# The bias table left raw, loaded first, and six of its rows made on GpSimd

## The chip, the cores and the metric

The kernel runs on one core of one Trainium2 chip. The metric is the device time of one execution in microseconds (us), lower is better. The core has five engines that run on their own and meet at semaphores: TensorE (PE, with its weight loads PEld), VectorE (DVE), ScalarE (ACT), GpSimd (POOL) and SyncE (SP, which here only issues DMAs).

## The reference

Three blocks run one after the other: attention with a learned relative bias, and two mixer blocks. The change is in the bias alone, so only that part of the reference matters:

```python
# q, k, v: [4, 8, 576, 64]; hidden = 32
pos = np.arange(S)
rel = (pos[:, None] - pos[None, :]).astype(np.float32)
psi_rel = np.log1p(np.abs(rel))
psi_i = np.log1p(np.maximum(pos[:, None].astype(np.float32), 1.0))
x = (psi_rel / psi_i)[..., None]
h = np.maximum(x @ w1 + b1, 0.0)        # [576, 576, 32]
bias = h @ w2                           # [576, 576, 8 heads]
scores = scores + bias.transpose(2, 0, 1)[None, :, :, :]
# softmax over the last axis, times v, then the two mixer blocks
```

For one query row the hidden layer is 32 units by 576 keys. Four query rows fill the 128 partitions.

## The kernel before, in words

A row's logarithms log(1+|i-j|) are a slice of one table, `ttab` (128 partitions by 1152), since they depend on i-j alone. Division by psi_i > 0 is taken out of the maximum: the kernel makes max(w1*t + b1*psi_i, 0) and scales it afterwards. `times_w1` (L311) first turns the table into -w1*t in place, once for the first 640 columns and once for the other 512. Then `hidden(gi)` makes a group of 16 query rows as four tiles X of 128x576, four rows each: three on VectorE as min(-w1*t, b1*psi_i) (L347; the sign and the constant are put right afterwards), the fourth on ScalarE as a true Relu (L349). `bias_product` (L366) multiplies them by w2 on TensorE, eight matmuls into one PSUM tile `bps`; `bias_place` (L379) scales the tile by `over_c` and adds `evb` on ScalarE, and a DMA (L385, L389) carries it to `bias_m` or `bias_t`, where the scores read it. X tiles lie in 12 slots that are used in turn, so a tile waits for the matmuls that read its slot three groups before.

There are 36 groups, in the order of `groups` (the four of the last 64 rows first). Six are made ahead of the attention (loop over `GUP`), between the transposes of k (L398 to L403). The other 30 are spread over the loop `single(n)`, two in each step from n = -3 to n = 11. In step n TensorE does: `ss`, the scores of unit n+3 (L470); transposes z, x and y of unit n (L525, L546, L551); a transposition of q into the `bps` buffer (L425); the products of two groups (L366); `values` of unit n-1 (L570 to L577). VectorE does in step n: `pr` (L476: scores plus bias, and the row minimum `mn`), a reciprocal (L496), a second `pr`, the three X tiles of a group, a copy of y (L556), the three X tiles of a second group, and the add of the values (L451). ScalarE does the exponentials (L489), two `bst` (L379), a copy of q (L435), two X tiles (L349) and copies of z and x. GpSimd adds the epsilon to the row sums (L495) and divides by them (L503: `pr` in one instruction of 576 or in three of 576, 64 and 512). In the steps from -3 to 10 the tiles of the groups 2n+14 and 2n+15 are made, one step ahead of their products.

The order of the work on each engine is the order in which the code is written (a manual schedule); SP issues all DMAs in that order too. The score tiles `ss` and the `bps` tiles share two PSUM buffers: the transposition of q (L425) waits until VectorE has read the first `ss` tile of the step, and the second half of `ss` until ScalarE has emptied the last `bps`.

At the start SP loads `wsm` (w1, b1, w2 and psi_i, 77 KB), then `ttab`'s first 640 columns, then the rest. VectorE multiplies psi_i by b1 (L308) and the table by -w1. TensorE meanwhile multiplies zeros (L230). GpSimd builds the w2 operands and `one_row` (L315 to L329), which the products that give `evb` and `over_c` (L594, L598) wait for.

Of the kernel before, what the change touches and what calls it, by code (L numbers as in the profile page):

```python
# [7 lines left out]
F32 = mybir.dt.float32  # L8
F32R = mybir.dt.float32r
I32 = mybir.dt.int32  # L10
AF = mybir.ActivationFunctionType
ALU = mybir.AluOpType
# [7 lines left out]
def kernel(ctx, tc, ins, consts, out, dbg=None, nb=4, stop=None):  # L20
    nc = tc.nc
    V, S, G, T, D = nc.vector, nc.scalar, nc.gpsimd, nc.tensor, nc.sync

    q, k, v = ins["q"], ins["k"], ins["v"]
    B, H, N, HD = q.shape
    P = 128
# [158 lines left out]
    scale = -1.0 / float(HD) ** 0.5  # L185
# [3 lines left out]
    groups = [it * P // 16 + j for it in order0 for j in range((P if it < NM else TL) // 16)]  # L189
# [22 lines left out]
    first = tc.alloc_tile_pool(name="first", bufs=1, side="right")  # L212


    def spare(t):
        blk = t // ND % 3
        return X[:, t % ND, N * (1 + blk):N * (2 + blk)]

    warm = first.tile([P, 1], F32, name="warm")
    V.memset(warm, 0.0)  # L220
    S.activation(out=warm, in_=warm, func=AF.Exp)

    ND0, WN = 2, 512
    NQ = 2
    NV = (-2, -1, 0, 1)
    zero = first.tile([P, N], F32, tag="st", name="zero", bufs=4)[:, 0:WN]
# [6 lines left out]
    wsm = first.tile([P, SMALL], F32, name="wsm")  # L233
    ttab = first.tile([P, 2 * N], F32, name="ttab")
    TC, SM = N + TL, 2 + H + NI
    D.dma_start(out=wsm[:, 0:SM], in_=consts["tab"][:, 0:SM])
    D.dma_start(out=ttab[:, 0:TC], in_=consts["tab"][:, SMALL:SMALL + TC])
    w1c, b1c = wsm[:, 0:1], wsm[:, 1:2]
    pi, rp = wsm[:, 2 + H:2 + H + NI], wsm[:, 2 + H + NI:SMALL]
    D.dma_start(out=ident, in_=consts["ident"])  # L240
# [45 lines left out]
    def load_q0(it):  # L286
        i = order0.index(it)
        if i < NM:
            t = raw_p.tile([P, N], F32, tag=("kr", "qr")[i % 2], name="qm", bufs=1)
        else:  # L290
            t = first.tile([P, DM], F32, name="qm")
        t = t[:, 0:DM].rearrange("p (h d) -> p h d", h=H)
        w = P if it < NM else TL
        D.dma_start(out=t[0:w], in_=q[0, :, it * P:it * P + w, :].rearrange("h p d -> p h d"))
        for p in range(NP):
            qraw[0, p, it] = t[0:w, 2 * p:2 * p + 2].rearrange("p h d -> p (h d)")
# [3 lines left out]
        out=ktail0[0:TL], in_=k[0, :, NM * P:N, :].rearrange("h p d -> p h d")  # L300
# [6 lines left out]

    V.tensor_scalar_mul(out=pi, in0=pi, scalar1=b1c)  # L308

    def times_w1(j):  # L310
        V.tensor_scalar(out=ttab[:, j], in0=ttab[:, j], scalar1=w1c, scalar2=-1.0, op0=ALU.mult, op1=ALU.mult)  # L311

    times_w1(slice(0, TC))
    w2b = first.tile([P, 4, H], F32, name="w2b")
    G.memset(w2b, 0.0)  # L315
    for g in range(4):
# [6 lines left out]
        out=w2r[:, 0:3].rearrange("k c g h -> k (c g) h"),  # L323
        in_=wsm[0:HID, 2:2 + H].rearrange("k (o h) -> k o h", o=1).to_broadcast([HID, 12, H]),
# [5 lines left out]
    rps = ps_t.tile([P, NI // 4], F32, tag="z", name="rps")  # L330
    over_c = first.tile([P, NI // 4], F32, name="over_c")
    evp = ps_t.tile([P, 1], F32, tag="o", name="evp")
    evb = first.tile([P, 1], F32, name="evb")

    nhid = [0]

    def hidden(gi):

        hs = []
        for c in range(4):  # L340
            hd = spare(nhid[0])
            nhid[0] += 1
            base = N - 1 - 16 * gi - 4 * c
            tt = ttab[:, base:base + N]
            b1i = pi[:, 4 * gi + c:4 * gi + c + 1]
            if c < 3:
                V.tensor_scalar(out=hd, in0=tt, scalar1=b1i, scalar2=None, op0=ALU.min)  # L347
            else:
                S.activation(out=hd, in_=tt, func=AF.Relu, scale=-1.0, bias=b1i)  # L349
            hs.append(hd)  # L350
        return hs

# [9 lines left out]
    def bias_product(gi, hs, ps=None):  # L362
        ps = s_tile("bps") if ps is None else ps
        for c in range(4):
            for hf in range(2):
                T.matmul(  # L366
                    ps[32 * c:32 * c + 32, hf, 0:HN],
                    lhsT=w2b.rearrange("p g h -> p (g h)"),
                    rhs=hs[c][:, hf * HN:(hf + 1) * HN],
                    start=True, stop=True, tile_position=(0, 32 * c),  # L370
                )
        return ps

    def bias_place(gi, ps):
        if gi in early:
            st = early.pop(gi)
        else:
            st = first.tile([P, N], F32, tag="st", name="bst", bufs=4)
        S.activation(  # L379
            out=st.rearrange("p (a n) -> p a n", a=2), in_=ps[:, :, 0:HN], func=AF.Identity, scale=over_c[:, gi:gi + 1],  # L380
            bias=evb,
        )
        i0 = 16 * gi
        if i0 < NM * P:
            D.dma_start(out=bias_m[i0 % P // 16:P:GT, i0 // P], in_=st)  # L385
        else:
            r0 = i0 - NM * P
            for a in range(2):
                D.dma_start(out=bias_t[a * TL + r0 // 16:(a + 1) * TL:TL // 16], in_=st[a:P:2])  # L389

    def k_parts0(p, pool, tag):

        m, tl = kraw.pop((0, p))
        tl = tl[0:TL, 2 * p:2 * p + 2]
        yk = ps_t.tile([P, NM, P], F32, tag="xy"[p % 2], name="yk")
        xk = ps_t.tile([P, TL], F32, tag="zo"[p % 2], name="xk")
        for t in range(NM):
            T.transpose(yk[:, t], m[:, t], ident)  # L398
        T.transpose(xk, tl.rearrange("p h d -> p (h d)"), ident[0:TL, 0:TL])
        kt = pool.tile([P, N], F32, tag="kt" + tag, name="kt", bufs=2)  # L400
        M = NM * P
        S.copy(out=kt[:, 0:M].rearrange("d (p t) -> d p t", t=NM), in_=yk.rearrange("d t p -> d p t"))
        V.tensor_copy(out=kt[:, M:N], in_=xk)  # L403
        keys[0, p] = kt
# [15 lines left out]
    def q_turn(n, zq):  # L420

        b, p, it = units[n]
        w = P if it < NM else TL
        if b == 0:
            T.transpose(zq[:, 0:w], qraw.pop((b, p, it)), ident[0:w, 0:w])  # L425
        else:
            queries[n] = turned(b, p)[:, it * P:it * P + w]

    def q_out(n, zq):
        b, p, it = units[n]  # L430
        if b > 0:
            return
        w = P if it < NM else TL
        t = hl_p.tile([P, P], F32, tag="q0", name="q0", bufs=5)[:, 0:w]
        S.copy(out=rows(t, w), in_=dealt(zq[:, 0:w], w))  # L435
        queries[n] = t
# [152 lines left out]
    def hide(gi):  # L589
        if gi < GALL:  # L590
            hs[gi] = hidden(groups[gi])
# [3 lines left out]
        evp, lhsT=w2r.rearrange("k c g h -> k (c g h)"), rhs=b1c[0:HID], start=True, stop=True  # L595
# [4 lines left out]
            tile_position=(0, 32 * c),  # L600
        )
    hide(1)
    V.tensor_scalar_mul(out=evb, in0=evp, scalar1=-1.0 / scale)
    V.tensor_scalar_mul(out=over_c, in0=rps, scalar1=1.0 / scale)
    hide(2)

    for gi in range(GUP):
        if gi == NQ:
            load_q0(order0[1])
        if gi == 2:  # L610
            times_w1(slice(TC, 2 * N))
        if gi > 0:
            bias_place(groups[gi - 1], bps)
            hide(gi + 2)
        bps = bias_product(gi, hs.pop(gi))
        if gi >= GUP - NP:
            p = gi - (GUP - NP)
            k_parts0(p, hl_p if p < 2 else first, "" if p < 2 else "x")
        if gi >= GUP - 2:
            u = gi - (GUP - 2)  # L620
            zq = ps_t.tile([P, P], F32, tag="z", name="zq")
            q_turn(u, zq)
            q_out(u, zq)
    bias_place(groups[GUP - 1], bps)
    gnext = GUP

# [97 lines left out]
    def single(n):  # L724
# [22 lines left out]
        for gi, ps in zip(gs, bp):  # L747
            bias_place(groups[gi], ps)
            if gi == gs[0]:
                q_out(n + 5, zq)  # L750
# [367 lines left out]
    with tc.tile_pool(name="sgw", bufs=1, reuse_waits="tile") as sw, tc.tile_pool(  # L1118
        name="sg", bufs=1, reuse_waits="tile"
# [313 lines left out]
```

## Time and profile before

| | |
|---|---|
| median of 3 runs | 873.35 us (873.16 to 873.83) |
| the profiled execution: its time | 873.12 us |
| its span in the profile | 871.2 us |
| busy PE / PEld / DVE / ACT / POOL | 99% / 88% / 71% / 48% / 26% of the span |
| granted TensorE clock, mean | 1.00 |

1.92 us of the profiled execution lie outside the span. The busy shares are means over unlike stages: the bias groups are made in the first 92 us, where all of VectorE, ScalarE and TensorE are close to full, while the mixers after 300 us are TensorE's alone. The part that the change touches is therefore read in stretches of 5 to 20 us, and by which engine each one waits for.

### The profile page before, as it was taken

To read this page: it belongs to the slowest core of one execution; us is meant where nothing else is said; L and a number is where in the kernel's file an instruction comes from. 1 tells how busy PE (TensorE), PEld (TensorE's weight loads), DVE (VectorE), ACT (ScalarE), POOL (GpSimd) and SP (SyncE) were. 2 spreads that over 40 slices of the span, in tenths; PEclk is the share of its full clock that TensorE was granted. 3 is DMA by queue.
4 is the path that set the end of the run, shared out by engine and by line. 5 is a ranking of instruction groups with operands and counts; after the bars stand their busy time and mean duration, and the time that the engine had idled before them with its cause. 6 is when DMAs were issued, how large, how long until landed. Compare 5 with 4: busy or idle time off the path is not lost.

```text
span 871.2 us, 22145 instructions
## 1 busy us (share of the span) xinstructions
PE 861.0 (99%) x8962; PEld 763.8 (88%) x8962; DVE 622.5 (71%) x1429; ACT 420.5 (48%) x955; POOL 229.5 (26%) x440
## 2 busy tenths in 40 slices
PE   9999999999999999999999999999999999999998
PEld 4466788888888898999999999999998989889996
DVE  7899788888887689899735353422118989887756
ACT  7999888888888634343322121211115522322310
POOL 1345567676767200000000000000002512322230
PEclk9999999999999999999999999999999999999999
DMA  7965554444432222243402001000051001010002
GB/s 191 197 137 130 126 101 78 80 96 90 82 72 59 62 66 82 73 124 118 122 1 73 25 25 44 6 1 0 1 83 49 26 0 50 2 60 2 1 13 96
DMA packets 123990, 57.55 MB, mean 66 GB/s; under 512 B 104177, under 2 KB 112497, under 8 KB 123889
## 3 DMA queue, kind: packets, MB, share of 16 engines
q1 hardware_dynamic: 123728, 56.01, 26.6%
q8 instruction: 70, 1.15, 0.5%
q14 instruction: 32, 0.25, 0.1%
q10 hardware_dynamic: 160, 0.13, 0.1%
HBM read 38.62 MB, written 4.72 MB: 50 GB/s over the span
## 4 chain that ended last, share of the span: by engine, by line
PE 86%; DVE 9%; ACT 2%; issue 1%; DMA 1%; SPq 0%; DVEq 0%; ACTq 0%
PE a L1064 17%; PE pg L900 17%; PE ss L470 9%; PE pu L1231 5%; PE o L570 5%; PE ps L1253 5%; PE po L1284 4%; PE pv L1178 4%; PE x L546 4%; PE y L551 3%; PE bps L366 3%; PE o L571 2%; PE z L525 2%; PE pu L932 1%; PE ph L646 1%
## 5 line engine op out<-in xcount | busy, mean ns | idle before, releaser
L1064 PE MATMUL a<-g,c 128*128 128x384 f32 x864 | 161.5, 334 | 0.0
L1064 PEld LDWEIGHTS a<-g,c 128*128 128x128 f32 x864 | 151.1, 188 | 0.0
L907 DVE SCALAR_TENSOR_TENSOR g<-pg,g 128x384 fp32r<-128x384 f32 x72 | 40.0, 556 | 146.7 <-ACT g L906 146.7
L503 POOL TENSOR_SCALAR pr<-pr,sm 128x576 f32<-128x576 f32 (+2 forms) x208 | 129.8, 640 | 47.0 <-DVE sm L496 38.8
L900 PE MATMUL pg<-u,c 128*128 128x384 f32 x720 | 134.5, 334 | 0.0
L900 PEld LDWEIGHTS pg<-u,c 128*128 128x128 f32 x720 | 125.7, 188 | 0.1
L906 ACT ACTIVATE g<-pg 128x384 fp32r<-128x384 f32 x72 | 35.3, 491 | 182.5 <-PE pg L900 175.0
L489 ACT ACTIVATE pr<-pr,mn 128x576 f32<-128x576 f32 x144 | 112.2, 780 | 6.7 <-DVE mn L476 4.5
L476 DVE CUSTOM_DVE_ANT_0 pr<-ss,bias_m 128x576 f32<-128x576 f32 x128 | 94.5, 749 | 19.4 <-PE ss L470 17.0
L62 POOL TENSOR_TENSOR y<-X,y 128x576 fp32r<-128x576 f32 x4 | 6.1, 1543 | 362.2 <-ACT y L61 362.2
L570 PEld LDWEIGHTS o<-xA,vm 64*64 64x64 f32 x1280 | 69.9, 133 | 11.2 <-issue 5.6
L570 PE MATMUL o<-xA,vm 64*64 64x128 f32 (+1 forms) x1280 | 78.8, 261 | 0.0
L1019 DVE STREAM_TRANSPOSE res<-X 32x256 f32<-32x256 f32 (+1 forms) x176 | 68.2, 387 | 2.9
L571 PE MATMUL o<-yA,vm 64*64 64x128 f32 x1024 | 68.0, 272 | 0.0
L470 PE MATMUL ss<-kt,X 64*64 64x288 f32 x816 | 66.8, 410 | 0.0
L132 ACT ACTIVATE sq<-wraw 128x512 f32<-128x512 f32 (+2 forms) x43 | 27.9, 650 | 68.2 <-DVE w L149 56.5
L571 PEld LDWEIGHTS o<-yA,vm 64*64 64x64 f32 x1024 | 56.4, 133 | 0.4
L1253 PE MATMUL ps<-wsT,vn 128*128 128x288 f32 x384 | 56.4, 295 | 0.0
L347 DVE TENSOR_SCALAR X<-ttab,wsm 128x576 f32<-128x576 f32 x108 | 55.4, 573 | 0.1
L1253 PEld LDWEIGHTS ps<-wsT,vn 128*128 128x128 f32 x384 | 52.7, 188 | 0.3 <-POOL vn L62 0.3
L1231 PE MATMUL pu<-y,wi 128*128 128x288 f32 x384 | 51.8, 295 | 1.0 <-ACT uT L1235 1.0
L1231 PEld LDWEIGHTS pu<-y,wi 128*128 128x128 f32 x384 | 51.3, 188 | 1.6 <-ACT uT L1235 1.3
(170 smaller groups left out, 1661.1 us busy)
## 6 DMA issues: line engine op xcount, KB each, us to landing
wraw<-in_moe_w_ch_dram SPq DMA_DIRECT2D x24, 512.0 KB, 3.6
bias_m<-bst SPq DMA_DIRECT2D x32, 288.0 KB, 3.9
vm<-in_v_dram SPq DMA_DIRECT2D x32, 128.0 KB, 3.1
wraw<-in_moe_w_in_dram SPq DMA_DIRECT2D x8, 512.0 KB, 3.6
out_dram<-res SPq DMA_DIRECT2D x16, 256.0 KB, 2.0
kr<-in_k_dram SPq DMA_DIRECT2D x48, 72.0 KB, 2.5
qr<-in_q_dram SPq DMA_DIRECT2D x48, 72.0 KB, 2.4
wraw<-in_moe_w_out_dram SPq DMA_DIRECT2D x4, 512.0 KB, 3.4
```

The costliest lines, as they stand in the source:

```text
L347: V.tensor_scalar(out=hd, in0=tt, scalar1=b1i, scalar2=None, op0=ALU.min)
L470: T.matmul(ss[a % na][o, hf, 0:HN], lhsT=ql, rhs=kr_, start=True, stop=True)
L476: V.tensor_tensor_reduce(out=pr[:, a * NB:a * NB + N].rearrange("p (f n) -> p f n", f=2), in0=ss[a][:, :, 0:HN], in1=bias[a].rearrange("p ...
L489: S.activation(out=pr[:, a * NB:a * NB + N], in_=pr[:, a * NB:a * NB + N], func=AF.Exp, scale=-1.0, bias=mn[:, a:a + 1], accum_out=sm[:, a ...
L503: G.tensor_scalar(out=pr[:, dc:dc + hi - lo], in0=pr[:, lo:hi], scalar1=sm[:, a:a + 1], scalar2=1.0, op0=ALU.mult, op1=ALU.mult,)
L570: T.matmul(o[0:HD, 0:w], lhsT=vm[r, t, 0], rhs=xs[r, t, 0:w], start=st_, stop=en)
L571: T.matmul(o[HD:P, 0:w], lhsT=vm[r, t, 1], rhs=rh[r], start=st_, stop=en)
L900: T.matmul(pg, lhsT=c1[f][i][:, d], rhs=u[j][:, d], start=d == 0 and n == 0, stop=d == ND - 1 and n == 2)
L1019: V.transpose(out=o, in_=src(c)[32 * a:32 * a + 32])
L1064: T.matmul(acc[d], lhsT=c2[f][i][:, d * P:(d + 1) * P], rhs=g[j], start=f == f0 and n == 0, stop=f == f1 and n == 2,)
L1231: T.matmul(pu[:, hf, 0:HN], lhsT=wi[i][:, d, f * P:(f + 1) * P], rhs=y[j][:, d, js], start=d == 0 and m == 0, stop=d == ND - 1 and m == 2,)
L1253: T.matmul(ps[:, hf, 0:HN], lhsT=vn[i][:, t, ds_], rhs=wsT[j][:, t, js], start=t == 0 and m == 0, stop=False,)
```

## The change

The table is no longer multiplied by -w1. A small tile `nw1` = -w1 takes the place of `times_w1`, and each X tile on VectorE is made in one instruction from the raw table: multiply by `nw1`, then minimum with b1*psi_i. The Relu on ScalarE takes w1 as its scale. At the start the table's first columns are the first DMA on SP, and `wsm` goes out on ScalarE's own queue ahead of its table load. For six groups, at positions 9, 11, 13, 15, 17 and 19 of `groups`, the fourth tile is made on GpSimd with the same multiply and minimum as the first three; `evb` has a second column and six columns of `over_c` change their sign for the last 32 partitions, both on GpSimd, so that the placing comes out the same.

```diff
@@ -216,11 +216,7 @@
         blk = t // ND % 3
         return X[:, t % ND, N * (1 + blk):N * (2 + blk)]
 
-    warm = first.tile([P, 1], F32, name="warm")
-    V.memset(warm, 0.0)
-    S.activation(out=warm, in_=warm, func=AF.Exp)
-
-    ND0, WN = 2, 512
+    ND0, WN, GP = 2, 512, 9
     NQ = 2
     NV = (-2, -1, 0, 1)
     zero = first.tile([P, N], F32, tag="st", name="zero", bufs=4)[:, 0:WN]
@@ -233,8 +229,11 @@
     wsm = first.tile([P, SMALL], F32, name="wsm")
     ttab = first.tile([P, 2 * N], F32, name="ttab")
     TC, SM = N + TL, 2 + H + NI
-    D.dma_start(out=wsm[:, 0:SM], in_=consts["tab"][:, 0:SM])
     D.dma_start(out=ttab[:, 0:TC], in_=consts["tab"][:, SMALL:SMALL + TC])
+    S.dma_start(out=wsm[:, 0:SM], in_=consts["tab"][:, 0:SM])
+    warm = first.tile([P, 1], F32, name="warm")
+    V.memset(warm, 0.0)
+    S.activation(out=warm, in_=warm, func=AF.Exp)
     w1c, b1c = wsm[:, 0:1], wsm[:, 1:2]
     pi, rp = wsm[:, 2 + H:2 + H + NI], wsm[:, 2 + H + NI:SMALL]
     D.dma_start(out=ident, in_=consts["ident"])
@@ -307,10 +306,8 @@
 
     V.tensor_scalar_mul(out=pi, in0=pi, scalar1=b1c)
 
-    def times_w1(j):
-        V.tensor_scalar(out=ttab[:, j], in0=ttab[:, j], scalar1=w1c, scalar2=-1.0, op0=ALU.mult, op1=ALU.mult)
-
-    times_w1(slice(0, TC))
+    nw1 = first.tile([P, 1], F32, name="nw1")
+    V.tensor_scalar_mul(out=nw1, in0=w1c, scalar1=-1.0)
     w2b = first.tile([P, 4, H], F32, name="w2b")
     G.memset(w2b, 0.0)
     for g in range(4):
@@ -330,7 +327,8 @@
     rps = ps_t.tile([P, NI // 4], F32, tag="z", name="rps")
     over_c = first.tile([P, NI // 4], F32, name="over_c")
     evp = ps_t.tile([P, 1], F32, tag="o", name="evp")
-    evb = first.tile([P, 1], F32, name="evb")
+    evb = first.tile([P, 2], F32, name="evb")
+    by_pool = groups[GP:GP + 12:2]
 
     nhid = [0]
 
@@ -343,10 +341,11 @@
             base = N - 1 - 16 * gi - 4 * c
             tt = ttab[:, base:base + N]
             b1i = pi[:, 4 * gi + c:4 * gi + c + 1]
-            if c < 3:
-                V.tensor_scalar(out=hd, in0=tt, scalar1=b1i, scalar2=None, op0=ALU.min)
+            if c < 3 or gi in by_pool:
+                eng = V if c < 3 else G
+                eng.tensor_scalar(out=hd, in0=tt, scalar1=nw1, scalar2=b1i, op0=ALU.mult, op1=ALU.min)
             else:
-                S.activation(out=hd, in_=tt, func=AF.Relu, scale=-1.0, bias=b1i)
+                S.activation(out=hd, in_=tt, func=AF.Relu, scale=w1c, bias=b1i)
             hs.append(hd)
         return hs
 
@@ -378,7 +377,7 @@
             st = first.tile([P, N], F32, tag="st", name="bst", bufs=4)
         S.activation(
             out=st.rearrange("p (a n) -> p a n", a=2), in_=ps[:, :, 0:HN], func=AF.Identity, scale=over_c[:, gi:gi + 1],
-            bias=evb,
+            bias=evb[:, 1:2] if gi in by_pool else evb[:, 0:1],
         )
         i0 = 16 * gi
         if i0 < NM * P:
@@ -600,15 +599,18 @@
             tile_position=(0, 32 * c),
         )
     hide(1)
-    V.tensor_scalar_mul(out=evb, in0=evp, scalar1=-1.0 / scale)
+    V.tensor_scalar_mul(out=evb[:, 0:1], in0=evp, scalar1=-1.0 / scale)
     V.tensor_scalar_mul(out=over_c, in0=rps, scalar1=1.0 / scale)
+    G.tensor_copy(out=evb[:, 1:2], in_=evb[:, 0:1])
+    G.tensor_copy(out=evb[3 * 32:P, 1:2], in_=evb[2 * 32:3 * 32, 0:1])
+    for gi in by_pool:
+        o = over_c[3 * 32:P, gi:gi + 1]
+        G.tensor_scalar(out=o, in0=o, scalar1=-1.0, scalar2=1.0, op0=ALU.mult, op1=ALU.mult)
     hide(2)
 
     for gi in range(GUP):
         if gi == NQ:
             load_q0(order0[1])
-        if gi == 2:
-            times_w1(slice(TC, 2 * N))
         if gi > 0:
             bias_place(groups[gi - 1], bps)
             hide(gi + 2)
```

On VectorE at the start of the program, before (`wsm` holds the scalars, `ttab` the table, X a hidden tile, `evb` and `over_c` the constants of the placing, kt a transposed k):

```order
L308 TENSOR_SCALAR wsm<-wsm 128x144
L311 TENSOR_SCALAR ttab<-ttab,wsm 128x640
L347 TENSOR_SCALAR X<-ttab,wsm 128x576 x6
L603 TENSOR_SCALAR evb<-evp 128x1
L604 TENSOR_SCALAR over_c<-rps 128x36
L347 TENSOR_SCALAR X<-ttab,wsm 128x576 x6
L311 TENSOR_SCALAR ttab<-ttab,wsm 128x512
L347 TENSOR_SCALAR X<-ttab,wsm 128x576 x3
L403 COPY kt<-xk 128x64
```

and the same place now (`nw_127` is nw1):

```order
L307 TENSOR_SCALAR wsm<-wsm 128x144
L310 TENSOR_SCALAR nw_127<-wsm 128x1
L346 TENSOR_SCALAR X<-ttab,nw_127,wsm 128x576 x6
L602 TENSOR_SCALAR evb<-evp 128x1
L603 TENSOR_SCALAR over_c<-rps 128x36
L346 TENSOR_SCALAR X<-ttab,nw_127,wsm 128x576 x9
L402 COPY kt<-xk 128x64
```

Both passes over the table are gone from VectorE, one instruction on a single column has come, and every X reads a third operand.

On ScalarE in steps -3 to -1 of the loop, before (q is a turned block of queries):

```order
L489 ACTIVATE pr,sm<-pr,mn 128x576
L379 ACTIVATE bst<-bps,evb,over_c 128x576
L435 COPY q_345<-bps 128x64
L379 ACTIVATE bst<-bps,evb,over_c 128x576
L349 ACTIVATE X<-ttab,wsm 128x576 x2
L489 ACTIVATE pr,sm<-pr,mn 128x576
L379 ACTIVATE bst<-bps,evb,over_c 128x576
L435 COPY q_393<-bps 128x64
L379 ACTIVATE bst<-bps,evb,over_c 128x576
L349 ACTIVATE X<-ttab,wsm 128x576 x2
```

and now:

```order
L488 ACTIVATE pr,sm<-pr,mn 128x576
L378 ACTIVATE bst<-bps,evb,over_c 128x576
L434 COPY q_353<-bps 128x64
L378 ACTIVATE bst<-bps,evb,over_c 128x576
L348 ACTIVATE X<-ttab,wsm 128x576
L488 ACTIVATE pr,sm<-pr,mn 128x576
L378 ACTIVATE bst<-bps,evb,over_c 128x576
L434 COPY q_401<-bps 128x64
L378 ACTIVATE bst<-bps,evb,over_c 128x576
L348 ACTIVATE X<-ttab,wsm 128x576
```

One of the two X tiles between the second `bst` and the next exponential is gone.

On GpSimd after `one_row`, before (sm is the row sums, pr a tile of exponentials):

```order
L495 TENSOR_SCALAR sm<-sm 128x1
L503 TENSOR_SCALAR pr<-pr,sm 128x576
L495 TENSOR_SCALAR sm<-sm 128x1
L503 TENSOR_SCALAR pr<-pr,sm 128x576
L495 TENSOR_SCALAR sm<-sm 128x1
L503 TENSOR_SCALAR pr<-pr,sm 128x576
```

and now:

```order
L604 COPY evb<-evb 128x1
L605 COPY evb<-evb 32x1
L608 ISA
L608 TENSOR_SCALAR over_c<-over_c 32x1 x6
L346 TENSOR_SCALAR X<-ttab,nw_127,wsm 128x576
L494 TENSOR_SCALAR sm<-sm 128x1
L502 TENSOR_SCALAR pr<-pr,sm 128x576
L346 TENSOR_SCALAR X<-ttab,nw_127,wsm 128x576
L494 TENSOR_SCALAR sm<-sm 128x1
L502 TENSOR_SCALAR pr<-pr,sm 128x576
```

Eight small instructions come first, and in each step one X tile stands between a division and the next epsilon.

## Rows read from the trace of the kernel before

**Rows 1.** The chain that ended last, first 5 us: start, length, what.
```profile
1.18 2.98 DMA ttab<-const_tab_dram
```

**Rows 2.** Timeline, first 9 us: start, length, engine, line, tile, idle before, releaser.
```profile
0.72 0.39 SPq L236 DMA_DIRECT2D wsm<-const_tab_dram  x1
...
2.71 0.30 DVE L308 TENSOR_SCALAR wsm<-wsm 128x144 f32<-128x144 f32 x1 [1.29 <-DMA wsm<-const_tab_dram]
...
4.78 2.67 DVE L347 TENSOR_SCALAR X<-ttab,wsm 128x576 f32<-128x576 f32 x6
...
5.18 0.58 PE L594 MATMUL evp<-wsm,zA 32*128 32x1 f32 x2
...
7.71 0.83 ACT L379 ACTIVATE bst<-bps,evb,over_c 128x576 f32<-128x576 f32 x1 [0.83 <-DVE over_c L604]
...
8.60 1.00 PEld L366 LDWEIGHTS bps<-X,w2b 128*32 128x32 f32 x16 [0.46 <-ACT bst L379]
```

**Rows 3.** Lines L311, L1212, L347 (to 18, 22 to 36 us): ns, min/median/max.
```profile
L311 DVE TENSOR_SCALAR ttab<-ttab,wsm x2: 477/515/553, 4.2 to 10.1; 128x640 f32<-128x640 f32 x1, 128x512 f32<-128x512 f32 x1
...
L1212 DVE TENSOR_SCALAR v<-v,mv,n x18: 536/542/1545, 676.4 to 824.0; 128x512 f32<-128x512 f32 x18
...
L347 DVE TENSOR_SCALAR X<-ttab,wsm x24: 509/515/521, 4.8 to 15.8; 128x576 f32<-128x576 f32 x24
...
L347 DVE TENSOR_SCALAR X<-ttab,wsm x18: 497/508/1004, 23.2 to 33.5; 128x576 f32<-128x576 f32 x18
```

**Rows 4.** VectorE and ScalarE groups by shape: busy us, mean ns of one.
```profile
L133 DVE TENSOR_SCALAR w<-wraw 128x512 int32<-128x512 int32 x38 | 16.0, 422 | 0.0
...
L349 ACT ACTIVATE X<-ttab,wsm 128x576 f32<-128x576 f32 x36 | 26.3, 774 | 3.3 <-DVE ttab L311 3.3
...
L61 ACT CAST y<-X 128x576 fp32r<-128x576 f32 x16 | 9.9, 670 | 0.1
```

**Rows 5.** Timeline, 19 to 37 us: VectorE, GpSimd and one exponential.
```profile
19.25 2.67 DVE L347 TENSOR_SCALAR X<-ttab,wsm 128x576 f32<-128x576 f32 x6
22.41 0.76 DVE L476 CUSTOM_DVE_ANT_0 pr<-ss,bias_t 128x576 f32<-128x576 f32 x1 [0.50 <-PE ss L470]
23.17 3.14 DVE L347 TENSOR_SCALAR X<-ttab,wsm 128x576 f32<-128x576 f32 x6
23.35 0.94 POOL L503 TENSOR_SCALAR pr<-pr,sm 128x576 f32<-128x576 f32 x1 [2.67 <-DVE sm L496]
...
30.84 0.08 DVE L476 DVE_READ_ACCUMULATOR2_ANT mn<- 128x1 f32 x1
31.34 0.79 ACT L489 ACTIVATE pr<-pr,mn 128x576 f32<-128x576 f32 x1
35.20 0.76 DVE L476 CUSTOM_DVE_ANT_0 pr<-ss,bias_m 128x576 f32<-128x576 f32 x1 [1.23 <-ACT X L349]
36.14 0.74 POOL L503 TENSOR_SCALAR pr<-pr,sm 128x576 f32<-128x576 f32 x1 [3.41 <-DVE sm L496]
```

**Rows 6.** Busy time in stretches: stretch, its length, then each engine.
```profile
20.00:30.00 10.00, 9.26 (x109) 4.28 (x100) 9.50 (x23) 9.95 (x20) 2.70 (x5) 1.00 0.74 171
60.00:80.00 20.00, 20.00 (x367) 13.90 (x359) 19.80 (x48) 19.59 (x44) 9.62 (x22) 1.00 0.47 115
```

**Rows 7.** Timeline, steps 1 to 5: VectorE's waits, and TensorE's L425.
```profile
40.27 0.22 DVE L451 TENSOR_TENSOR X<-o,X 128x64 f32<-128x64 f32 x1 [0.93 <-ACT X L450]
40.67 0.76 DVE L476 CUSTOM_DVE_ANT_0 pr<-ss,bias_m 128x576 f32<-128x576 f32 x1 [0.18 <-PE ss L470]
45.73 0.23 DVE L451 TENSOR_TENSOR X<-o,X 128x64 f32<-128x64 f32 x1 [0.36 <-ACT X L450]
46.13 0.76 DVE L476 CUSTOM_DVE_ANT_0 pr<-ss,bias_m 128x576 f32<-128x576 f32 x1 [0.17 <-PE ss L470]
57.79 0.08 DVE L476 DVE_READ_ACCUMULATOR2_ANT mn<- 128x1 f32 x1
58.04 0.27 PE L425 MATMUL bps<-ident,qm 128*128 128x128 f32 x1
```

## The prediction

> **What bounds the kernel now.** I read the chain of waits first, for the stage in which the change lies; then the busy times in stretches; then the timeline of VectorE, ScalarE and GpSimd; then the durations of single lines, for the prices.
>
> At the start the chain is a load and then VectorE: the table's first columns arrive 2.98 us after their issue [rows 1], are multiplied, and at 4.78 the first six X tiles begin; only after these is `over_c` made, for which ScalarE's first `bst` waits 0.83 us, and for that `bst` TensorE's weight loads wait 0.46 us until 8.60 [rows 2]. From there TensorE goes through its list to the first scores nearly without a gap, so what this point gains or loses is carried on.
>
> In the loop three engines are full at once. From 20 to 30 us ScalarE is busy for 9.95 of 10 us and VectorE for 9.50; from 60 to 80 us TensorE for all 20, VectorE for 19.80 and ScalarE for 19.59 [rows 6]. VectorE's idle time behind the X tiles of a step says where it has room. In step -3 that is 0.50 us, before the `pr` at 22.41; then X tiles and `pr` follow each other without a wait until 35.20, where it has waited 1.23 us [rows 5]. In step 1 it has 0.93 and 0.18, in step 2 0.36 and 0.17 [rows 7], in step 3 the same as in step 2, and from step 4 to step 10 only the 0.20 us in 20 of the stretch [rows 6], that is 0.055 in a step of some 5.5 us (40.67 to 46.13, rows 7). After step 11 no X tile is left and TensorE bounds the rest of the span by itself. So the question is what the change adds to VectorE in the steps -3 to 10, and what the start gains.
>
> **The start.** The table's load moves from second to first on SP: its issue starts at 0.72 instead of 1.18 [rows 1, 2], and it lands near 3.70 instead of 4.16 if `wsm` on the other queue takes nothing from it. `wsm` was there 2.0 us after its issue (0.72 to 2.71, rows 2); now both run at once. Best case: first X at 3.75. Worst case: the two interleave so that both land near 4.1, and then come 0.30 us for psi_i (row of 2.71) and some 0.15 for `nw1`: first X at 4.6. I take 4.0, nearer to the first, since the load's price alone is a row. `times_w1` (0.55) is gone from between. The six X are now longer by 0.06 each (below), 0.36 together. The first `bst` came 2.93 after the first X (4.78 to 7.71); now 4.0 + 2.93 + 0.36 = 7.29, 0.4 earlier. It can't win more than about 0.65: TensorE is with its zeros until 5.18 [rows 2], whatever VectorE does, and the first product follows. At the other end 4.6 + 3.29 = 7.89, 0.2 later. The second `times_w1` (0.48) lies where TensorE's transposes and products set the pace, and I give it nothing; the eight small GpSimd instructions fall into that stretch too, on an engine that then has nothing to do, and cost nothing unless they hold up a VectorE X, which the bound of 0.2 covers. The start gains 0.4.
>
> **The second pointer.** Each X on VectorE now reads two per-partition scalars instead of one. The trace has all three forms at about this size: with two immediates 128x512 takes 422 ns (L133, rows 4), with one pointer 477 (the shorter L311), with two 542 (L1212, median of 18) [rows 3]. That is 55 and 65 ns for a pointer; I take 60. L1212 also keeps the speed of the others over the columns, so no slower mode is to be expected. Six X in a step: 0.36 us.
>
> **GpSimd's X tiles.** One takes about the 0.74 us of a division that has GpSimd to itself (36.14, rows 5), and GpSimd has the time: it is busy for 2.70 of 10 us [rows 6]. But VectorE pays. In step -3, with no division running, six X take 2.67 us; in step -2, with one division of 576 columns in the middle, 3.14 [rows 5]. One X of the six is stretched from 508 to 1004 ns [rows 3]: 0.50 us per division. The new X tile on GpSimd stands right behind the epsilon or the division, when VectorE is in its six X in each of the steps -3 to 2, so each costs 0.50; bounds 0 (it slips into a `pr`, beside which the 0.74 was measured) and 0.74. The Trainium skill (SBUF — State Buffer, Who interferes with whom) says that GpSimd and a VectorE instruction that uses both ports lock each other out for a whole instruction; the stretched X agrees in kind, and the measured 0.50 is less than the whole 0.74. By the rule's whole instruction the steps -3, -2, -1 and 2 would add 0.24 each, and the sum below would be 877.7.
>
> **What ScalarE gets.** It loses one X (774 ns, rows 4) in each of six steps. This helps only where an exponential waits for ScalarE rather than for VectorE: the one at 31.34 found its minimum ready at 30.92 [rows 5], so 0.40 us. The X tiles that stay get a pointer for their scale as well; L349 with one pointer takes 774, a cast of the same size without any 670 [rows 4], so some 0.10 more each, 0.20 in a step from 3 on, against 0.11 of idle time there (19.59 of 20, rows 6). The lengthening of VectorE's step covers it; without that it would cost 0.1 in a step.
>
> **The sum,** as delay of the point that sets the end: step -3 adds 0.36 + 0.50 and has 0.50 of idle time: 0.36. Steps -2 and -1 add 0.86 each with none: 2.08. In step 0 the 0.40 of ScalarE comes off: 1.68; by VectorE's own list it is 2.08 + 0.86 - 1.23 = 1.71. I go on with 1.7. Step 1 adds 0.86 and has 1.11: still 1.7. Step 2 adds 0.86 and has 0.53: 2.03. Step 3 adds 0.36 and has 0.53: 2.03. Steps 4 to 10 add 7 x (0.36 - 0.055) = 2.13, of which TensorE takes up 0.17 once (the minimum is there at 57.87, L425 starts at 58.04, rows 7): 1.96. Together 3.99, less the start's 0.4: 3.6. Nothing gives it back later, as TensorE has no idle time to lose. The profiled execution took 873.12 (0.23 under the median of 873.35): 873.12 + 3.6 = 876.7.
>
> With the upper ends (0.74, 65 ns, a start 0.2 later) the same sum is 2.89 - 0.40 + 0.02 + 0.60 + 2.18 + 0.2 = 5.5: 878.6. With nothing for pointer and lock: -0.40 and -0.65: 872.1.
>
> **Rivals.** First: the second pointer costs nothing. L1212 works in place and mostly stands alone in its list, so its 60 ns could be latency that a queue of X tiles hides. Then step -3 adds nothing, steps -2 and -1 0.50 each, less 0.40 is 0.6, the later idle times swallow the rest, and the start takes 0.4 off: 873.3, no change. Against it: 422, 477 and 542 are a regular series, and with one pointer the X in their queue take the 515 ns that the two L311 alone give for 576 columns between 477 and 553 [rows 3]. The Trainium skill (VectorE: DVE Perf Modes, the TRN2 errata) prices a VectorE instruction by its columns and a fixed latency, with nothing for scalars, and so stands with this rival; the three durations speak against it.
>
> Second, on the other side: ScalarE is the engine that bounds the steps -3 to 2, and VectorE has room in its queue that the busy time doesn't show. Then each of the six steps is shorter by an X of 0.77: 4.6, and 0.4 at the start: 868.1. For it: 9.95 of 10 [rows 6]. Against it: VectorE has no idle time between 22.41 and the wait before 35.20. It decides at the exponentials: they must start when ScalarE is free and not when the minimum arrives. If only the one at 31.34 does, and VectorE pays nothing, it is 872.1 as above, no change.
>
> Third: with the second pointer the X drop out of the fast mode. At double the time over the columns, some 0.3 us for 576 (from 553 - 477 = 76 ns for 128 columns, rows 3), 1.8 in a step, 14 steps are 25 us less some 4 of idle time: near 894. L1212's 542 is against it.
>
> **How the numbers follow.** Forecast 0.65, between 875.4 and 878.6; first rival 0.20; second 0.12, of which 0.09 under 871.6 and 0.03 near 872.1; third 0.03. A change below 0.2% (1.75 us) can't be told from none. Slower: 0.65 + 0.03 = 0.68; same: 0.20 + 0.03 = 0.23; faster: 0.09. The range 872.5 to 878.6 leaves out the fast and the slowest ends.
>
> **What would show it.** Right: the X of L346 take about 570 ns; in steps -3 to 2 one X more is stretched to about 1 us; VectorE has no idle time before the `pr` of steps -1 to 10, and those of steps 5 to 10 are 5.8 us apart instead of 5.5; TensorE's L425 waits for the minimum. The first `bst` starts near 7.3 and the first scores 0.4 earlier than before. Wrong: X of 510 ns, or steps of 5.5 throughout; or `wsm` landing so late that GpSimd's operands hold up the first product.

## The result and the profile after

The changed kernel takes 878.66 us (877.80 to 879.62, 4 runs) beside 873.25 (872.96 to 873.83, 4 runs) of the kernel before: ratio 1.0061, 95% interval 1.0049 to 1.0073. It is 0.6% slower. The forecast of 876.7 was 2 us too low: the time lies at the top end of the forecast's range (878.6; the median is 0.06 above it). The profiled execution took 878.60, with a span of 876.8 against 871.2.

Where the 5.6 us of span come from can be seen at a few points of the program that both kernels have: the first scores `ss`, and the first `pr` behind the X tiles of a step.

| point | before | after | delay | forecast |
|---|---|---|---|---|
| first scores | 17.29 | 19.25 | 1.96 | -0.4 |
| `pr` after step -3 | 22.41 | 24.46 | 2.05 | 0.0 |
| `pr` after step -1 | 30.16 | 34.77 | 4.61 | 1.7 |
| `pr` after step 0 | 35.20 | 39.73 | 4.53 | 1.3 |
| `pr` after step 3 | 51.59 | 56.25 | 4.66 | 1.6 |
| `pr` after step 10 | 90.22 | 95.50 | 5.28 | 3.6 |

So 2 us are lost before the loop, 2.6 in the steps -3 to 0, and only 0.6 in the steps 4 to 10, where the forecast had put the most. The 0.3 that come behind step 10 are no more than executions of one kernel differ by.

The timeline of the first 13 us of the kernel after, cut where `...` stands (start, length, engine, line, tile, idle time before it and what ended that; line numbers are those of the kernel after, some 1 to 4 lower than before):

```profile
0.73 0.39 SPq L232 DMA_DIRECT2D ttab<-const_tab_dram  x1
0.73 0.41 ACTq L233 DMA_DIRECT2D wsm<-const_tab_dram  x1
...
4.11 0.30 DVE L307 TENSOR_SCALAR wsm<-wsm 128x144 f32<-128x144 f32 x1 [2.72 <-DMA wsm<-const_tab_dram]
4.22 1.41 POOL L315 COPY w2b<-wsm 32x8 f32<-32x8 f32 x4 [3.37 <-DMA wsm<-const_tab_dram]
...
4.50 3.04 DVE L346 TENSOR_SCALAR X<-ttab,nw,wsm 128x576 f32<-128x576 f32 x6
...
5.67 0.53 POOL L318 MEMSET zA<- 32x128 f32 x1
6.27 0.41 POOL L319 COPY zA<-wsm 32x96 f32<-32x96 f32 x1
...
6.73 0.38 PE L593 MATMUL evp<-wsm,zA 32*128 32x1 f32 x2 [1.50 <-POOL zA L319]
...
7.29 4.84 PE L365 MATMUL bps<-X,w2b 128*32 128x288 f32 x48
...
8.65 0.83 ACT L378 ACTIVATE bst<-bps,evb,over_c 128x576 f32<-128x576 f32 x1 [1.83 <-PE bps L365]
...
12.05 0.66 PE L397 MATMUL yk<-ident,kraw 128*128 128x128 f32 x4
```

`wsm` is there at 4.1 and not at 2.7 [rows 2]. The DMA issues of the first 6 us (KB, us from issue to landing) show that the small load, on a queue of its own, lands behind the large one:

```profile
ttab<-const_tab_dram SPq DMA_DIRECT2D x1, 320.0 KB, 3.2
...
wsm<-const_tab_dram ACTq DMA_DIRECT2D x1, 77.0 KB, 3.4
```

VectorE doesn't mind much (first X at 4.50, before 4.78). But GpSimd makes `w2b` and `zA` from `wsm`, all that TensorE's first matmuls read, and now does it beside VectorE's X tiles. TensorE, done with its zeros, waits 1.50 us and starts its first matmul at 6.73, before at 5.18 [rows 2]. `yk`, the first transpose of k behind the first 48 products, comes at 12.05, and in the kernel before at 10.06:

```profile
10.06 0.66 PE L398 MATMUL yk<-ident,kraw 128*128 128x128 f32 x4
```

The loop, VectorE of the kernel after:

```profile
21.17 3.37 DVE L346 TENSOR_SCALAR X<-ttab,nw,wsm 128x576 f32<-128x576 f32 x6
24.46 0.74 DVE L475 CUSTOM_DVE_ANT_0 pr<-ss,bias_t 128x576 f32<-128x576 f32 x1
...
25.51 0.16 DVE L495 RECIPROCAL sm<-sm 128x1 f32<-128x1 f32 x1 [0.30 <-POOL sm L494]
25.59 4.30 DVE L346 TENSOR_SCALAR X<-ttab,nw,wsm 128x576 f32<-128x576 f32 x6
29.81 0.74 DVE L475 CUSTOM_DVE_ANT_0 pr<-ss,bias_t 128x576 f32<-128x576 f32 x1
```

and GpSimd beside it:

```profile
22.38 2.83 POOL L346 TENSOR_SCALAR X<-ttab,nw,wsm 128x576 f32<-128x576 f32 x1 [11.14 <-ACT pr L488]
25.29 0.19 POOL L494 TENSOR_SCALAR sm<-sm 128x1 f32<-128x1 f32 x1
25.78 0.99 POOL L502 TENSOR_SCALAR pr<-pr,sm 128x576 f32<-128x576 f32 x1 [0.30 <-DVE sm L495]
26.77 2.80 POOL L346 TENSOR_SCALAR X<-ttab,nw,wsm 128x576 f32<-128x576 f32 x1
```

The GpSimd tile takes 2.8 us, not 0.74. The epsilon (L494) stands in GpSimd's list behind it and keeps VectorE's reciprocal waiting; the division (L502) and the next tile then lie beside nearly all of the six X, which take 4.30 where the kernel before has 3.14 [rows 5]. The groups by line (ns, min/median/max) show the X themselves:

```profile
L346 DVE TENSOR_SCALAR X<-ttab,nw,wsm x108: 556/574/1074, 4.5 to 94.8; 128x576 f32<-128x576 f32 x108
...
L346 POOL TENSOR_SCALAR X<-ttab,nw,wsm x6: 2804/2818/2937, 22.4 to 48.3; 128x576 f32<-128x576 f32 x6
```

An X on VectorE is 0.06 longer, as priced [rows 3].

ScalarE, with one X less, waits for VectorE. The exponential behind the X tiles of step -2 starts only when VectorE has the row minimum `mn`:

```profile
30.59 0.78 ACT L488 ACTIVATE pr<-pr,mn 128x576 f32<-128x576 f32 x1 [2.14 <-DVE mn L475]
```

### The profile page after: what moved, and what is told of

The parts are those of the page before. It is cut to its first block, busy times and chain, and to the rows that moved or that the text cites. A ratio compares the mean times of both kernels' runs of the same rounds, so it can differ in the third digit from the quotient of the medians.

```text
span 876.8 us, 22148 instructions
## 1 busy us (share of the span) xinstructions
PE 862.5 (98%) x8962; PEld 763.7 (87%) x8962; DVE 629.8 (72%) x1428; ACT 420.3 (48%) x949; POOL 252.6 (29%) x454
## 4 chain that ended last, share of the span: by engine, by line
PE 85%; DVE 10%; ACT 1%; issue 1%; DMA 1%; POOL 1%; SPq 0%; ACTq 0%; DVEq 0%; POOLq 0%
PE a L1066 17%; PE pg L902 17%; PE ss L469 8%; PE pu L1233 5%; PE o L569 5%; PE ps L1255 5%; PE po L1286 4%; PE pv L1180 4%; PE x L545 3%; PE bps L365 3%; PE y L550 3%; PE o L570 2%; PE z L524 2%; PE pu L934 1%; DVE X L346 1%; PE ph L648 1%
## 5 line engine op out<-in xcount | busy, mean ns | idle before, releaser
L502 POOL TENSOR_SCALAR pr<-pr,sm 128x576 f32<-128x576 f32 (+2 forms) x208 | 130.1, 642 | 36.9 <-DVE sm L495 31.8
L346 DVE TENSOR_SCALAR X<-ttab,nw,wsm 128x576 f32<-128x576 f32 x108 | 64.0, 654 | 0.0
```

The costliest lines, as they stand in the source:

```text
L346: eng.tensor_scalar(out=hd, in0=tt, scalar1=nw1, scalar2=b1i, op0=ALU.mult, op1=ALU.min)
L502: G.tensor_scalar(out=pr[:, dc:dc + hi - lo], in0=pr[:, lo:hi], scalar1=sm[:, a:a + 1], scalar2=1.0, op0=ALU.mult, op1=ALU.mult,)
```

## Experiments

Theory A, from this reading: three parts that add up, the start (late `wsm`, TensorE waiting for GpSimd) 2.0, the GpSimd tiles 2.5, the second pointer under 1. Its rival is the prediction's own sum (start -0.4, tiles some 2, pointer some 2). Every ratio compares a run with the kernel before on the same chip, where its medians were 873.09 to 873.42; differences between two changed versions can cross chips. The cuts from the code show the lines that matter, shortened.

### The three parts

**load_old.** The changed kernel with the loads as before:

```
-    D.dma_start(out=ttab...)          +    D.dma_start(out=wsm...)
-    S.dma_start(out=wsm...)           +    D.dma_start(out=ttab...)
```

> The changed kernel with the loads in the old order: wsm first on SP, the table behind it. Theory A (three separate parts: the late wsm leaves TensorE idle at the start, worth about 2.0; the GpSimd X tiles of 2.8 us, worth about 2.5; the second pointer under 1): 878.7 - 2.0 = 876.7, first weight load of bst and first scores back near their old times. The prediction's own sum (the new order gains 0.4 at the start, the delay is made in the loop): 879.1. If GpSimd's late operands are not what counted but the GpSimd X tiles hide the start: no change, 878.7.

876.67 us, ratio 1.0039 (1.0025 to 1.0053), as theory A expected; first scores at 17.48.

**no_pool.** The changed kernel with `by_pool = []`.

> The changed kernel without the X tiles on GpSimd: ScalarE makes every fourth row. Theory A: the steps -3 to 2 no longer gain delay beyond the start's 2.0, so 878.7 - 2.3 = 876.4, with the later steps as in the changed kernel. The prediction's sum (0.50 for each tile, of which some is covered): only about 0.7 less, 878.0. If ScalarE was relieved by more than GpSimd's tiles cost: above 878.7.

875.58 us, 1.0025 (1.0014 to 1.0036): below both expectations. The 878.0 put down to the prediction doesn't follow from its sum, either: without the tiles only the 1.96 of the steps 4 to 10 are left of its 3.99, so it gives some 2.0 less, near 876.6.

**ptr_only.** Both edits, so that the raw table and the pointer alone are left.

> The changed kernel with the loads in the old order and no X tile on GpSimd: the raw table and the second pointer alone. Theory A: the steps 5 to 10 stay 5.5 long and the pointer costs under 1 us in all: 873.3 to 874.1. The prediction's sum (0.36 a step, no room in the steps 4 to 10): 1.96 there, and some 0.4 before: 875.6.

874.08 us, 1.0012 (1.0003 to 1.0020), at the upper end of theory A's range and 1.5 under the prediction's. The pointer that ScalarE's X get and the two products of the table that are gone count in here too.

**load_only.** The kernel before with the new loads alone.

> The kernel before with the new order of loads alone (the table still multiplied by VectorE, no second pointer, no X tile on GpSimd). Theory A: TensorE waits for GpSimd's operands as in the changed kernel, first product near 7.2 instead of 5.8, a granted clock under 1.00 behind it, and about +2 at the end: 875.3. The prediction's account of the start (both loads only shift VectorE): within 0.2 of 873.3.

875.21 us, 1.0025 (1.0015 to 1.0035), as theory A expected; first product at 7.55, first scores at 19.22.

From the kernel before to ptr_only, load_old and the changed kernel there is 1.0 for the pointer, 2.6 for the tiles (876.67 - 874.08) and 2.0 for the loads (878.66 - 876.67). That these three make 5.6, with 5.4 measured, tests nothing, since each is the step from one run to the next. The test is the same edit beside other ones: the loads cost 2.1 alone, 1.5 beside the pointer (875.58 - 874.08) and 2.0 beside pointer and tiles; the tiles cost 2.6 with the old loads and 3.1 with the new. So the parts add up to within some 0.6. Theory A holds to that extent, and each term of the forecast is off, the first by its sign.

One expectation of theory A stays open: TensorE's clock. Behind the wait the kernel after has a granted clock of 0.50, the level of 1.2 GHz, from 9 to 11 us; load_only, behind as long a wait (1.67), has 1.00. In stretches (length, then busy time of PE, PEld, DVE, ACT, POOL, then the clock), kernel after:

```profile
9.00:11.00 2.00, 2.00 (x22) 1.08 (x18) 2.00 (x5) 1.86 (x3) 2.00 (x5) 0.50 0.83 189
```

and load_only:

```profile
9.00:11.00 2.00, 2.00 (x28) 0.96 (x24) 1.61 (x5) 1.13 (x2) 0.00 (x0) 1.00 0.72 163
```

But the products themselves are long in both. From 9 to 10 us (ns, min/median/max), kernel after and then load_only:

```profile
L365 PE MATMUL bps<-X,w2b x13: 684/684/687, 8.5 to 10.0; 128*32 128x288 f32 x13
```

```profile
L365 PE MATMUL bps<-X,w2b x16: 627/687/687, 8.5 to 10.0; 128*32 128x288 f32 x16
```

In the kernel before, and in both of these from 14.5 us on, the median is 406. So the granted clock of load_only doesn't show how fast its products ran, and the two traces can't be set against each other as one with and one without the low clock.

Both reach `yk` at the same time (12.05 and 12.03), but the 2 us are not idle time alone. In the kernel after the first `bst` is 0.94 late (8.65, before 7.71 [rows 2]) and `yk` 1.99; the other 1.05 arise in between, where the products are long. There the chain that ended last, which in the kernel before runs over VectorE's X tiles, lies on TensorE's products:

```profile
7.48 4.64 PE bps L365 x48
```

What the wait would cost with products of 406 ns no run shows, nor what made them long: load_old and w2_act (next) have some of 687 ns too, from 5.8 us on, without the wait.

### The start: what waits for wsm

**w2_act.** In the changed kernel, ScalarE makes the copies:

```
-        G.tensor_copy(out=w2b[r, g, :], in_=wsm[r, 2:2 + H])
+        S.copy(out=w2b[r, g, :], in_=wsm[r, 2:2 + H])
```

> The changed kernel with the four small copies of w2b made by ScalarE, which waits for wsm anyway, instead of GpSimd. Theory A (the start is lost because GpSimd gets wsm late and then makes everything that TensorE's first matmuls read): zA is ready near 4.7, TensorE goes on from its zeros at 5.2 and the first bps product comes near 5.9 instead of 7.29; 878.7 - 1.8 = 876.9. If something else in the new load order costs the 2 us (the k and x loads, the ScalarE queue): no change, 878.7.

876.37 us, 1.0035 (1.0021 to 1.0049): 2.3 less than the change (0.5 under the 876.9 expected), and no more than with the old loads (876.67). Its timeline:

```profile
4.05 0.81 ACT L315 COPY w2b<-wsm 32x8 f32<-32x8 f32 x4 [1.38 <-DMA wsm<-const_tab_dram]
4.10 0.30 POOL L319 COPY zA<-wsm 32x96 f32<-32x96 f32 x1 [3.13 <-DMA wsm<-const_tab_dram]
...
5.15 0.58 PE L593 MATMUL evp<-wsm,zA 32*128 32x1 f32 x2
...
5.81 3.49 PE L365 MATMUL bps<-X,w2b 128*32 128x288 f32 x36
```

`wsm` is as late as in the changed kernel, and TensorE starts at 5.15 all the same. So the loss is not the late load by itself; it takes the six small GpSimd instructions (four copies, a memset and the copy of `zA`) that then lie between it and TensorE. Here ScalarE has the four copies, and the memset is done at 0.78, long before the load.

### The GpSimd tile: why 2.8 us

**forms.** One execution of load_old, with the six tiles in six forms, so that five of them leave out what the bias needs. The code is shortened, and the fifth tile also reads the table's first columns:

```
+   s1 = (nw1, b1i, nw1, nw1, nw1, -1.0)[k];  s2 = (b1i, 1.0, 1.0, b1i, b1i, 0.5)[k]
+   o0, o1 = mult min | min mult | mult mult | mult mult | mult min | mult min
```

> The changed kernel with the loads in the old order and its six GpSimd X tiles in six forms, in the order of the program: 0 mult by the pointer nw1, then min with the pointer b1i (as in the change); 1 min with b1i, then mult by 1.0; 2 mult by nw1, then mult by 1.0 (the form of the divisions); 3 mult by nw1, then mult by b1i; 4 as 0 but from the table's first columns; 5 mult by -1.0, then min with 0.5 (no pointer). Tiles 1 to 5 thus hold other numbers than the bias needs. If min is what makes 2.8 us: 2.8 in 0, 1, 4 and 5, near 0.74 in 2 and 3. If the second pointer: 2.8 in 0, 3 and 4, near 0.74 in 1, 2 and 5. If the source's place in the table: near 0.74 in 4 alone. If GpSimd is slow only because VectorE's X tiles run beside it (the prediction's lock, turned round): above 2 in all six.

**forms2.** One execution with six more:

> As the first run of forms, with six others, in the order of the program: 0 min with b1i alone; 1 mult by nw1, then max with b1i; 2 mult, then add b1i; 3 mult, then subtract b1i; 4 max with 0.0, then mult by 1.0; 5 is_gt 0.0, then mult by -1.0. The tiles hold other numbers than the bias needs. If everything that compares is slow on GpSimd: 2.6 to 2.9 us in 0, 1, 4 and 5, near 1.0 in 2 and 3. If only min: max and is_gt near 1.0. If only products are quick: 2.6 or more in all six.

GpSimd's tiles in forms:

```profile
20.52 2.83 POOL L354 TENSOR_SCALAR X<-ttab,nw,wsm 128x576 f32<-128x576 f32 x1 [9.14 <-ACT pr L496]
...
24.91 2.74 POOL L354 TENSOR_SCALAR X<-ttab,wsm 128x576 f32<-128x576 f32 x1
...
29.78 0.94 POOL L354 TENSOR_SCALAR X<-ttab,nw 128x576 f32<-128x576 f32 x1
...
34.33 1.01 POOL L354 TENSOR_SCALAR X<-ttab,nw,wsm 128x576 f32<-128x576 f32 x1
...
39.72 2.95 POOL L354 TENSOR_SCALAR X<-ttab,nw,wsm 128x576 f32<-128x576 f32 x1 [0.83 <-PE bps L373]
...
45.73 2.67 POOL L354 TENSOR_SCALAR X<-ttab 128x576 f32<-128x576 f32 x1
```

and in forms2:

```profile
20.97 2.28 POOL L354 TENSOR_SCALAR X<-ttab,wsm 128x576 f32<-128x576 f32 x1 [9.13 <-ACT pr L498]
...
25.40 2.80 POOL L356 TENSOR_SCALAR X<-ttab,nw,wsm 128x576 f32<-128x576 f32 x1
...
30.34 1.01 POOL L356 TENSOR_SCALAR X<-ttab,nw,wsm 128x576 f32<-128x576 f32 x1
...
34.96 2.81 POOL L356 TENSOR_SCALAR X<-ttab,nw,wsm 128x576 f32<-128x576 f32 x1
...
40.49 2.81 POOL L356 TENSOR_SCALAR X<-ttab 128x576 f32<-128x576 f32 x1 [0.83 <-PE bps L375]
...
46.52 2.67 POOL L356 TENSOR_SCALAR X<-ttab 128x576 f32<-128x576 f32 x1
```

It is the operation. Products alone take 0.94 with one pointer and 1.01 with two; mult and add takes 1.01; whatever has min, max or is_gt in it takes 2.28 to 2.95, with pointers or without, from either place of the table. The quick and the slow ones lie beside the same X tiles of VectorE, so these don't make the difference. Subtract after mult, 2.81, fits none of forms2's three expectations together with the quick add. Apart from the forms of the change, pool_only and pool_fast, each ran once.

**pool_only.** The kernel before, with the fourth row of the six groups on GpSimd in a one-pointer form:

```
+            elif gi in by_pool:
+                G.tensor_scalar(out=hd, in0=tt, scalar1=b1i, scalar2=1.0, op0=ALU.min, op1=ALU.mult)
```

> The kernel before (table multiplied by VectorE, old loads, one pointer) with the fourth row of the six groups on GpSimd, as min with b1i and then mult by 1.0. Theory A with the second pointer as the cause of the 2.8 us: tiles near 0.74, no more than the prediction's price (0.50 on VectorE for each, less the relief of ScalarE): 873.1 to 874.5. Theory A with min as the cause: tiles of 2.8 us again and 1.5 to 2.6 more than before, 874.7 to 875.7.

Tiles of 2.61 to 2.76 us; 874.72 us, 1.0018 (1.0009 to 1.0026), 1.5 more than before. min is the cause here too, at the lower end of what was expected of it. That the shorter X of one pointer leave VectorE more room would explain this, but isn't shown.

**pool_fast.** load_old with the GpSimd tiles as products, which leaves out their min:

```
+                    G.tensor_scalar(out=hd, in0=tt, scalar1=nw1, scalar2=1.0, op0=ALU.mult, op1=ALU.mult)
```

> The changed kernel with the loads in the old order and all six GpSimd X tiles as mult by nw1, then mult by 1.0: the form of the divisions, so these tiles lack their min and hold other numbers. If the prediction's step for the tile was right in all but the duration (0.50 on VectorE for each tile of 0.74 to 1.0 us, less some relief of ScalarE), it lies 0.4 to 1.0 above the pointer alone: 874.5 to 875.1. If giving GpSimd a tile costs the same however short it is: 876.6, as with the min. If a short tile is a gain: under 874.1.

Tiles of 0.93 to 1.08 us; 875.21 us, 1.0021 (1.0012 to 1.0030): 1.1 above the pointer alone, 0.1 above the range expected, and 1.5 under load_old. VectorE's X tiles of step -2, first ptr_only:

```profile
23.50 3.45 DVE L346 TENSOR_SCALAR X<-ttab,nw,wsm 128x576 f32<-128x576 f32 x6
```

then pool_fast:

```profile
23.79 3.86 DVE L346 TENSOR_SCALAR X<-ttab,nw,wsm 128x576 f32<-128x576 f32 x6
```

A short tile stretches the six by 0.41; the forecast had 0.50. For this term the mechanism was right and the duration wrong: with tiles as short as assumed, the forecast's price would nearly have held.

### The second pointer: where it costs

**ptr_late** and **ptr_early.** The kernel before, with a second pointer (a column of ones, which changes no number) in the X tiles of some groups; `>= 22` for the late ones, `< 22` for the early ones:

```
+                if (nhid[0] - 1) // 4 >= 22:
+                    V.tensor_scalar(out=hd, in0=tt, scalar1=ones, scalar2=b1i, op0=ALU.mult, op1=ALU.min)
```

> The kernel before with a second pointer (a column of ones, mult, then min) in VectorE's X tiles from step 4 on alone; the start, the steps -3 to 3, ScalarE and GpSimd as before. Theory A (half of the longer X is taken up beside the division, and most of the rest by a wait before pr that the busy share hid): the X are 0.06 longer, the steps 5 to 10 stay 5.5 long, 873.2 to 873.4. The prediction's term for these steps: 1.96 more, 875.2.

873.37 us, ratio 1.0004 (0.9995 to 1.0013): no difference, where the forecast had 1.96.

> The complement: the second pointer (of ones) in VectorE's X tiles of the prologue and of the steps -3 to 3 alone, the table still multiplied ahead of them. Theory A: X tiles set the pace at the start and in the steps -2 and -1, so some 0.5 to 0.8 at the first scores (nothing is gained by the missing product here) and 0.3 to 0.4 more by step 0: 874.1 to 874.4. The prediction's terms for the pointer there: 0.36 at the start, nothing that lasts in step -3, 0.72 in steps -2 and -1, mostly swallowed by VectorE's 1.23 of idle time in step 0: 873.4 to 873.8.

874.80 us, 1.0018 (1.0009 to 1.0026): 1.4 more, above both expectations. First scores come at 18.68, 1.39 late.

Why nothing in the late steps: VectorE in step 10, the kernel before:

```profile
86.13 1.93 DVE L347 TENSOR_SCALAR X<-ttab,wsm 128x576 f32<-128x576 f32 x3
...
88.58 1.37 DVE L347 TENSOR_SCALAR X<-ttab,wsm 128x576 f32<-128x576 f32 x3
89.88 0.29 DVE L451 TENSOR_TENSOR X<-o,X 128x128 f32<-128x128 f32 x1
90.22 0.76 DVE L476 CUSTOM_DVE_ANT_0 pr<-ss,bias_m 128x576 f32<-128x576 f32 x1
```

and ptr_late:

```profile
86.50 1.93 DVE L350 TENSOR_SCALAR X<-ttab,ones,wsm 128x576 f32<-128x576 f32 x3
...
88.95 1.54 DVE L350 TENSOR_SCALAR X<-ttab,ones,wsm 128x576 f32<-128x576 f32 x3
90.42 0.28 DVE L456 TENSOR_TENSOR X<-o,X 128x128 f32<-128x128 f32 x1
90.61 0.74 DVE L481 CUSTOM_DVE_ANT_0 pr<-ss,bias_m 128x576 f32<-128x576 f32 x1
```

The three X beside the division take 1.93 either way: a longer X is stretched less. The other three take 0.17 more. Of that `pr` gives back 0.15: it starts 0.34 after L451's start before, and 0.19 after L456's here, laid over its end. The busy time counted L451 to its end and so showed a full engine where there was a small wait for scores.

The chain that ended last says the same of these steps. From 52 to 92 us it lies on TensorE alone in the kernel before (its shares by line), and in ptr_late too; VectorE, busy for 19.80 of 20 us there [rows 6], is not on it:

```profile
by line: PE bps L366 38.5%; PE ss L470 18.8%; PE o L570 15.2%; PE y L551 8.7%; PE x L546 8.5%; PE z L525 4.5%; PE bps L425 2.2%; PE o L571 1.8%; PE o L577 1.7%; PE o L580 0.3%
```

Why so much early: VectorE makes 24 X tiles up to 18 us [rows 3], and TensorE and ScalarE follow it. 24 times 0.06 is 1.44, close to the 1.39. In the changed kernel the two products of the table, 0.55 and 0.48 (the two L311, rows 3), are gone from the same list, so some 0.4 remains: in ptr_only the first scores come at 17.61, 0.32 late, though its first X starts 0.36 earlier (4.42).

### An attempt at a better kernel

**combo.** The kernel before with the new loads, the copies of `w2b` on ScalarE, the pointer only ahead of the loop, shorter zeros, and:

```
+    V.tensor_scalar_mul(out=over_c, ...)      (ahead of hide(1), not behind it)
+        if gi == GUP - 1:
+            times_w1(slice(0, 2 * N))
```

> An attempt at a better kernel from what the runs showed. From the kernel before: the new order of loads, w2b copied by ScalarE, the second pointer only for the groups before the loop and the whole table multiplied once just ahead of the loop, where VectorE is idle for 1.9 of 7 us; no X tile on GpSimd; over_c made ahead of the second group's X tiles, since bst(0) waited 0.83 for it; zeros of 384 columns in place of 512, so that TensorE is free near 4.3. Theory A: first product near 5.0 instead of 5.8, first scores 0.4 to 0.8 earlier, nothing lost in the loop: 872.4 to 872.9. If TensorE's own list or the loads of k bound the start: 873.3. If VectorE's longer list before the loop counts, or TensorE's clock falls: 873.5 to 875.

873.74 us, ratio 1.0005 (0.9996 to 1.0014): no gain. Theory A's 872.4 to 872.9 was wrong; the time lies in the range expected if VectorE's longer list before the loop counts. Its first product comes at 5.23 in place of 5.82, but the 48 products take 5.17 where they took 4.32, and the first scores come at 17.69. As ptr_early shows, X tiles set the pace there. No version here beats the kernel before.

## Why the prediction was right, and where it was wrong

The direction came out and the rough size too, in part by luck: the start came 2.4 worse than forecast and the tiles 0.6 to 1.1, the pointer 1.0 better, and the 2 us between forecast and time are what is left.

- **The start** (forecast 0.4 gained, measured 1.96 lost) is the step that failed. Its worst case, both loads interleaved to land near 4.1 and first X at 4.6, is what happened (4.1 and 4.50). What failed is the bound "At the other end 4.6 + 3.29 = 7.89, 0.2 later": it followed VectorE alone. `wsm` has a second reader, GpSimd, whose small copies TensorE waits for, and load_only and w2_act show that path to be worth 2, the wait and the long products behind it together. The prediction had the path in its description and named it as what would make it wrong, but gave it no time. It also counted six X for the longer tiles, where 24 set the pace (ptr_early), and gave the second product nothing, though VectorE made it in that same list.
- **The GpSimd tile** "takes about the 0.74 us of a division" failed: 2.8. The division row is a product, the tile has a min (forms). Its price on VectorE for a short tile was right, 0.41 beside 0.50 (pool_fast). The steps -3 to 0 lost 2.6 (4.53 - 1.91, from the first `pr`) instead of 1.7; step 2 added 0.05, where the forecast had 0.33.
- **The second pointer**, 60 ns, was right: X of 574 ns. "Steps 4 to 10 add 7 x (0.36 - 0.055)" failed: 0.0 by ptr_late. The busy share was taken for the room, while the chain of the kernel before lies on TensorE in these steps; steps of 5.5 us throughout were one of the prediction's own signs of being wrong. Of the 0.6 that the changed kernel does lose there, 0.43 come in step 5, where the three divisions start together with the first three X (63.16 and 63.23) and stretch them to 2.34 instead of 2.00.
- The X on ScalarE take 0.09 more (median 866 beside 774 ns) as estimated.
- Of the rivals, the first (the pointer is free) holds in the late steps and fails at the start, and the third (the slower mode) is refuted by the 574 ns. The second (ScalarE bounds the steps -3 to 2) was to be decided at the exponentials, and in the kernel after one of them waits 2.14 us for VectorE's minimum (30.59); in pool_only and pool_fast, where ScalarE also has six tiles less, the time rises too.
- The rule of the Trainium skill (SBUF — State Buffer, Who interferes with whom) would have one of the two engines wait for a whole instruction of the other. The 2.83 us tile at 22.38 runs beside the X tiles of step -3 until 24.46, for 2.1 us, and they take 3.37 where ptr_only has 3.02: 0.35, not 2.1. For VectorE, beside this tile, the trace does not bear the rule out; how much of the 2.83 is GpSimd's own waiting it doesn't tell.

## What to carry to other kernels

When a load is moved, follow every engine that reads it up to the bounding one, and not only the engine whose work was meant to start earlier: here six small instructions on GpSimd, behind a late load, were worth 2 us. Take the price of an instruction on GpSimd from a row with the same operation, since the shape and the number of operands told nothing. A busy share near 1 doesn't mean that there is no room (overlapped ends and stretched instructions count as busy): ask first which engine the chain that ended last lies on. And a stage that looks bound by TensorE may be paced by the engine that feeds it; adding 60 ns to each of that engine's instructions shows it.

## What the runs showed of the hardware

- GpSimd on 128x576 f32: mult and mult 0.94 to 1.01 us, mult and add 1.01; min alone 2.28, and min, max, is_gt or subtract beside a second operation 2.67 to 2.95.
- VectorE beside a GpSimd tile with min is held up by a fraction of the time (0.35 of 2.1), beside a short product by nearly half (0.41 of 0.94).
- 77 KB issued together with 320 KB, each on its own queue, took 3.4 us, and the 320 KB 3.2; issued first on the same queue, the 77 KB were there after 2.0.
- The granted clock fell to 0.50 behind a wait of 1.5 us in the profiled execution of the changed kernel and stayed at 1.00 behind one of 1.67 in load_only. The products of 288 columns took 684 and 687 ns all the same, and 406 later: a granted clock of 1.00 did not mean quick products there.
